# Retention and a low-rank mixer: the first two batches by pairs of heads, loads on two queues

## The chip, the cores and the metric

The kernel runs on one core of a Trainium2 chip. The time is the device time of one execution in microseconds. The core has a matrix engine (PE, whose weight loads are shown as PEld), a vector engine (DVE), a scalar engine (ACT), a general engine (POOL) and a sync engine (SP). Each takes its own instructions in program order, and they wait for one another by semaphores. DMAs are issued by SP, ACT or POOL and share 16 DMA engines.

## The reference

```python
B, H, S, D = 8, 8, 576, 64            # batch, heads, tokens, head width
scores = (1 / sqrt(D)) * q @ k^T
gamma  = 1 - 2 ** (-5 - h)            # one decay per head
ret    = scores * where(i >= j, gamma ** (i - j), 0)
x      = (ret @ v), heads side by side   # [B, S, 512]
h      = x^T @ U @ V                  # U [576, 32], V [32, 576]: mixes tokens
u      = x + h^T
out    = u + relu(u @ w_ch1) @ w_ch2  # w_ch1 [512, 2048], w_ch2 [2048, 512]
```

All inputs and the output are float32; the kernel computes its products in bf16.

## The kernel before

Retention runs by chunks of 128 tokens. Within a chunk k and q are transposed, scores are multiplied and masked (`ret`), and `ret @ v` goes to `po`; from chunk to chunk a state (sum of k^T v) is carried, which q is multiplied with. The decay is put into factors: v is scaled by gamma^-t (`vscale`) and the result by gamma^t (`qscale`) as x is written. 576 tokens are four and a half chunks, so two batches share nine chunks; the middle one, J, holds the last 64 tokens of the even batch and the first 64 of the odd one.

Then, for a batch: `a` = U^T x (MA), u^T (for batch 0 built as x^T plus V^T a; for the others as a transpose of u), u = x + h (MH), y1 = relu(u w_ch1) kept transposed, 16 blocks of four or five chunks (`Y1`, L477), and y2 = y1 w_ch2 plus u (`Y2`, L511), stored from POOL's queue.

Batches 2 to 7 are woven into the y1 and y2 of the batch before them by a fixed merge, and load, cast and transpose by DMA ahead of their use. The first two batches have a hand-written order instead, and only this order is touched:

- `startup` (L779) does batch 0 up to its u^T. The unit is 256 tokens with all eight heads; each tensor of a unit is two loads of 256 KB (four heads each), all from SP. A token pair lies side by side in a partition, so that k and q are transposed with even and odd tokens apart. POOL casts k and q to bf16 (L592) and scales v (L596). `T_u` transposes on PE, DVE or ACT copies; `SC_u` makes scores of four heads, `mask_u` masks them on DVE (L643); `ST_u` sums states, which ACT copies to `sblk` as block-diagonal pairs (L697); `RV_u` and `QS_u` add into `po`; `XS_u` writes x. `T_J`, `SC_J` and so on do the half chunk. At the end stand 16 x^T matmuls (L859), MA of all four 128-column blocks, four matmuls V^T a (L874) and the four copies to u^T (L882).
- `warm(n)` puts n matmuls on the identity, 512 columns wide, into the order; 21 in all.
- `early_consts` is called ahead of everything: identity, masks, decay factors; ACT computes three exponentials there.
- `first_stretch` (L886) then runs the 16 y1 items of batch 0 (`y(n)` gives n of them) with batch 1's two units between them, `MA1`, MH and the transposes `MT1`, and begins y1 of batch 1.

Buffers: stage (float32 loads) 15; in PSUM one buffer each for `psc`, `po` and `pss` (states, MA), and three for `big` (transposes, x^T, y1, y2). DMAs from SP and ACT use eight completion semaphores in turn, and an issue waits until the DMA eight before it in program order has landed.

Of the kernel before, what the change touches and what calls it, by code (L numbers as in the profile page):

```python
# [35 lines left out]
def kernel(  # L36
# [23 lines left out]
    J = 4  # L60
# [35 lines left out]
    vscaleU = consts.tile([P, 4, 2, H], FP32, name="vscaleU")  # L96
# [17 lines left out]
    def early_consts():  # L114
# [21 lines left out]
        nc.scalar.activation(out=vscaleU, in_=posU, func=AF.Exp, bias=lnb, scale=-1.0)  # L136
# [21 lines left out]
    def load_u_rows():  # L158
        nc.sync.dma_start(
            out=U_f[:, 0:4, :], in_=moe_U[0:4 * P, :].rearrange("(c p) r -> p c r", p=P))  # L160
        nc.sync.dma_start(out=U_f[0:HALF, J, :], in_=moe_U[4 * P:S, :])

    def load_v_rows():
        nc.sync.dma_start(out=V_f, in_=moe_V)

    def make_u():
        nc.scalar.activation(out=U_E[:, 0:J, :], in_=U_f[:, 0:J, :], func=AF.Copy)
        nc.scalar.activation(out=U_E[0:HALF, J, :], in_=U_f[0:HALF, J, :], func=AF.Copy)

        ps = ps_s.tile([P, 5, R], FP32, tag="pss", name="pu_o")  # L170
        nc.tensor.matmul(ps, swap, U_E, start=True, stop=True)
        nc.scalar.activation(out=U_O[0:HALF, 1:5, :], in_=ps[0:HALF, 0:4, :], func=AF.Copy)
        nc.scalar.activation(out=U_O[HALF:P, :, :], in_=ps[HALF:P, :, :], func=AF.Copy)
# [59 lines left out]
    def cast_qk(pr, i, rows=slice(0, P), eng=None):  # L233
# [4 lines left out]
        if eng is not None:  # L238
            for j in (1, 0):
                eng.tensor_copy(  # L240
                    out=t[rows, j, :], in_=c["f", j][rows].rearrange("p h d -> p (h d)"))
            return
# [222 lines left out]
    def y1_items(par, by_seg=False):  # L465
        nch = 4 + par
        segs = [(0, 4)] if par == 0 else [(0, 3), (3, 2)]
        items = []

        def Y1(f, seg):  # L470
            if f == 0 and seg == 0:
# [88 lines left out]
    un = [dict() for _ in range(4)]  # L560
    st["x", 0] = x_pool.tile([P, NI, dm], BF16, tag="x", name="xt")

    def unit_i0(u):
        return 2 * u + (1 if u >= 2 else 0)

    def load_u(u, which):
        b = u // 2
        t0 = 2 * P * (u % 2) + HALF * b
        for j in which:
            dram = (q, k, v)[j]  # L570
            for hh in range(2):
                t = stage.tile([P, H, D], FP32, tag="stage", name="stage_t")
                un[u]["f", j, hh] = t
                nc.sync.dma_start(  # L574
                    out=t.rearrange("p (h j) d -> p h (j d)", j=2),
                    in_=dram[b, 4 * hh:4 * hh + 4, t0:t0 + 2 * P, :].rearrange(
                        "h (p j) d -> p h (j d)", j=2),
                )

    def unit_views(u, j, hh):  # L580
        if j not in un[u]:
            un[u][j] = qk_pool.tile([P, 2, dm], BF16, tag="qk", name="qk")
        w = slice(hh * 4 * D, (hh + 1) * 4 * D)
        return (un[u][j][:, :, w].rearrange("p j (h d) -> p h j d", d=D),
                un[u]["f", j, hh].rearrange("p (h j) d -> p h j d", j=2))

    def cast_u(u, j, hh, eng):
        o, f = unit_views(u, j, hh)
        if eng is nc.scalar:
            nc.scalar.activation(out=o, in_=f, func=AF.Copy)  # L590
        else:
            eng.tensor_copy(out=o, in_=f)  # L592

    def scale_u(u, hh, eng):
        o, f = unit_views(u, 2, hh)
        eng.tensor_tensor(  # L596
            out=o, in0=f,
            in1=vscaleU[:, u, :, 4 * hh:4 * hh + 4].rearrange("p j h -> p h j")[
                :, :, :, None].to_broadcast([P, 4, 2, D]),
# [3 lines left out]
    def T_u(u, j, eng):  # L603
        pst = ps_big.tile([P, 2 * NHP, P], BF16, tag="big", name="pst")
        for jj in range(2):
            for hp in range(NHP):
                nc.tensor.transpose(
                    pst[:, jj * NHP + hp, :], un[u][j][:, jj, hp * P:(hp + 1) * P], ident)
        t = qkT_pool.tile([P, 2 * NHP, P], BF16, tag="qkT", name="qkT")
        un[u]["T", j] = t  # L610
        o, i_ = t, pst
        if j == 0:

            o = t.rearrange("p a b -> p (a b)").rearrange(
                "p (hp t j) -> p j hp t", hp=NHP, j=2)
            i_ = pst.rearrange("p (j hp) t -> p j hp t", j=2)
        if eng is nc.scalar:
            nc.scalar.activation(out=o, in_=i_, func=AF.Copy)
        else:
            eng.tensor_copy(out=o, in_=i_)  # L620

    def qT(u):
        return un[u]["T", 0].rearrange("p a b -> p (a b)").rearrange(
            "p (hp t) -> p hp t", hp=NHP)

    def SC_u(u, hh, pool_, tag):
        psc = pool_.tile([P, 2, NHP, P], FP32, tag=tag, name="psc")
        kT, qt = un[u]["T", 1], qT(u)
        for hp in range(2):
            for jj in range(2):  # L630
                for s in range(2):
                    for hl in range(2):
                        r = slice(hl * HALF, (hl + 1) * HALF)
                        m = slice(s * HALF, (s + 1) * HALF)
                        nc.tensor.matmul(  # L635
                            psc[m, hl, hp * 2 + jj, :], kT[r, jj * NHP + 2 * hh + hp, m],
                            qt[r, 2 * hh + hp, s * P:(s + 1) * P], start=True, stop=True,
                        )
        un[u]["psc", hh] = psc

    def mask_u(u, hh):
        ret = ret_pool.tile([P, H, P], BF16, tag="ret", name="ret")
        nc.vector.tensor_tensor(  # L643
            out=ret.rearrange("p (a j) i -> p a (j i)", j=2),
            in0=un[u]["psc", hh].rearrange("p a b i -> p (a b i)").rearrange(
                "p (a ji) -> p a ji", a=4),
# [3 lines left out]
        un[u]["ret", hh] = ret  # L650

    def RV_u(u, hh):
        if "po" not in un[u]:
            un[u]["po"] = ps_o.tile([P, 2, dm], FP32, tag="po", name="po")
        for hp in range(2):
            for hl in range(2):
                h = 4 * hh + 2 * hp + hl
                for jj in range(2):
                    for s in range(2):
                        r = slice(s * HALF, (s + 1) * HALF)  # L660
                        nc.tensor.matmul(  # L661
                            un[u]["po"][:, s, h * D:(h + 1) * D],
                            un[u]["ret", hh][r, hl * 4 + hp * 2 + jj, :],
                            un[u][2][r, jj, h * D:(h + 1) * D],
                            start=(h == 0 and jj == 0), stop=True, skip_group_check=True,
                        )

    def QS_u(u, s, slot):
        for hp in range(NHP):
            nc.tensor.matmul(  # L670
                un[u]["po"][:, s, hp * P:(hp + 1) * P],
                qT(u)[:, hp, s * P:(s + 1) * P], sblk[:, slot, hp, :],
                start=False, stop=True, skip_group_check=True,
            )

    def XS_u(u, c0=0, c1=2):
        i0, n = unit_i0(u) + c0, c1 - c0
        nc.vector.tensor_tensor(  # L678
            out=st["x", 0][:, i0:i0 + n, :].rearrange("p s (h d) -> p s h d", d=D),
            in0=un[u]["po"][:, c0:c1, :].rearrange("p s (h d) -> p s h d", d=D),  # L680
            in1=qscale[:, i0:i0 + n, :, None].to_broadcast([P, n, H, D]), op=ALU.mult,
        )

    def ST_u(u, rows, acc, start):
        for hp in range(NHP):
            for jj in range(2):
                nc.tensor.matmul(  # L687
                    acc[:, hp, :], un[u][1][rows, jj, hp * P:(hp + 1) * P],
                    un[u][2][rows, jj, hp * P:(hp + 1) * P],
                    start=(start and hp == 0 and jj == 0), stop=True,  # L690
                    skip_group_check=True,
                )

    def Sblk(acc, slot):
        for hl in range(2):
            r = slice(hl * HALF, (hl + 1) * HALF)
            nc.scalar.activation(  # L697
                out=sblk[r, slot, :, hl * D:(hl + 1) * D],
                in_=acc[r, :, hl * D:(hl + 1) * D], func=AF.Copy)

    LO, HI, ALL = slice(0, HALF), slice(HALF, P), slice(0, P)

    def T_J(r):
        c = ch[0, J]
        pst = ps_big.tile([P, 2 * NHP, P], BF16, tag="big", name="pst")
        for j in range(2):
            for hp in range(NHP):
                nc.tensor.transpose(
                    pst[:, j * NHP + hp, r], c["qk"][r, j, hp * P:(hp + 1) * P],
                    ident[r, r])  # L710
        if "qkT" not in c:
            c["qkT"] = qkT_pool.tile([P, 2 * NHP, P], BF16, tag="qkT", name="qkT")
        nc.scalar.activation(out=c["qkT"][:, :, r], in_=pst[:, :, r], func=AF.Copy)

    def SC_J(r):
        c = ch[0, J]
        c["psc"] = ps_sc.tile([P, 2, NHP, P], FP32, tag="psc", name="psc")
        for hp in range(NHP):
            for hl in range(2):
                d = slice(hl * HALF, (hl + 1) * HALF)  # L720
                nc.tensor.matmul(
                    c["psc"][r, hl, hp, r], c["qkT"][d, NHP + hp, r], c["qkT"][d, hp, r],
# [3 lines left out]
    def mask_J(r):  # L726
        c = ch[0, J]
        if "ret" not in c:
            c["ret"] = ret_pool.tile([P, H, P], BF16, tag="ret", name="ret")
        nc.vector.tensor_tensor(  # L730
            out=c["ret"].rearrange("p (hp hl) i -> p hl hp i", hl=2)[r, :, :, r],
            in0=c["psc"][r, :, :, r],
            in1=tri[r, None, None, r].to_broadcast([HALF, 2, NHP, HALF]), op=ALU.mult,
        )

    def RV_J(r):
# [277 lines left out]
```

## Time and profile before

| | |
|---|---|
| median of 3 runs | 335.97 us (334.06 to 337.58) |
| span of the profiled execution | 335.6 us, clock 0.974 on average |
| first y1 matmul of batch 0 starts | 32.1 us |
| first y1 matmul of batch 1 starts | 61.2 us |
| first y2 matmul | 82.1 us |
| idle of PE between 50 and 60, 60 and 70 us | 1.0, 1.2 us |
| PE busy from 100 us to the end | 231.1 of 235.6 us |

The span goes from the first to the last instruction of one profiled execution. A line of a timeline or chain gives start and length in us, engine, program line, operation, and output <- input; `x20` says that 20 instructions were merged, and the brackets at the end give idle time before it and what ended that. A line of windows gives a stretch, its length, busy time and instructions of PE, PEld, DVE, ACT and POOL, the granted PE clock (1.00 is full), the DMA engines' busy share and GB/s. `SPq` is SP's issuing of DMAs.

### The profile page before, as it was taken

The page shows a single profiled execution, that of the slowest core. Times are in us where ns is not written, and L with a number is a line of the kernel's source. Part 1 is how long each engine was busy: PE and PEld are TensorE (multiplying, and loading weights), DVE is VectorE, ACT ScalarE, POOL GpSimd, SP SyncE. Part 2 cuts the span into 40 slices and gives each one's busy share as a digit, 9 for nine tenths or more (in the row PEclk, how much of TensorE's full clock was granted, in tenths as well). Part 3 has the DMA queues.
Part 4 walks back from the last instruction along what each step waited for, and adds up shares of the span by engine and source line. Part 5 has one row for each costly group of instructions (what it writes and reads, how often), then busy time and mean ns, then how long its engine had stood idle before and what let it go on. Part 6 is the DMA issues. An engine that isn't in the chain of part 4 may idle for free.

```text
span 335.6 us, 6997 instructions
## 1 busy us (share of the span) xinstructions
PE 320.9 (96%) x2926; PEld 179.9 (54%) x2948; DVE 138.0 (41%) x190; ACT 139.2 (41%) x290; POOL 78.2 (23%) x112
## 2 busy tenths in 40 slices
PE   6688999899999999999999999999999999999996
PEld 3375554576544445446764455457754455457644
DVE  5453346433564234534356244524365144510022
ACT  2543665776210077107850176017740264037400
POOL 5686741211231140114102220222111100110000
PEclk9955999999999999999999999999999999999999
DMA  7999999999999929994998959995933400340012
GB/s 212 239 228 266 237 217 182 187 179 223 213 249 234 234 73 192 207 198 105 198 177 190 213 123 168 195 241 71 200 76 99 142 2 1 79 126 2 0 64 94
DMA packets 151311, 53.17 MB, mean 158 GB/s; under 512 B 131984, under 2 KB 148752, under 8 KB 151280
## 3 DMA queue, kind: packets, MB, share of 16 engines
q1 hardware_dynamic: 144512, 40.40, 64.7%
q0 software_dynamic: 6768, 12.32, 14.6%
q8 instruction: 23, 0.38, 0.5%
q14 instruction: 8, 0.07, 0.1%
HBM read 36.85 MB, written 9.44 MB: 138 GB/s over the span
## 4 chain that ended last, share of the span: by engine, by line
PE 91%; SPq 2%; issue 2%; DVE 2%; DMA 1%; ACT 1%; POOL 0%
PE ps_y L477 38%; PE ps_y L511 36%; PE psc L275 3%; PE po L314 2%; PE pss L687 2%; PE pss L340 2%; DMA stage_t<-in_q_dram 1%; SPq L574 1%; PE ph L421 1%; PE ps_y L522 1%; PE pa L394 1%; PE po L300 1%; PE po L661 1%; PE xT L859 1%; DVE xt L678 1%
## 5 line engine op out<-in xcount | busy, mean ns | idle before, releaser
L477 PE MATMUL ps_y<-uT,w_sb 128*128 128x256 bf16 (+2 forms) x768 | 137.0, 328 | 1.5 <-ACT uT L452 1.4
L482 ACT ACTIVATE y<-ps_y 128x384 bf16<-128x384 f32 (+2 forms) x192 | 90.0, 489 | 114.9 <-PE ps_y L477 114.2
L511 PE MATMUL ps_y<-w_sb,y 128*128 128x512 bf16 x538 | 124.3, 379 | 1.6 <-issue 0.8
L477 PEld LDWEIGHTS <-w_sb 128*128 128x128 bf16 x768 | 71.6, 98 | 46.7 <-issue 3.1
L511 PEld LDWEIGHTS <-y 128*128 128x128 bf16 x560 | 52.4, 98 | 60.3
L500 DVE TENSOR_TENSOR o_sb<-ps_y,u 128x512 f32<-128x512 f32 (+2 forms) x38 | 25.2, 663 | 76.6 <-PE ps_y L511 74.4
L503 POOL DMA_DIRECT2D out_dram<-o_sb x31 | 17.3, 558 | 158.6 <-DVE o_sb L500 152.8
L285 DVE TENSOR_TENSOR ret<-psc,tri 128x1024 bf16<-128x1024 f32 x24 | 29.4, 1225 | 47.3 <-PE psc L275 47.3
L254 POOL TENSOR_TENSOR vt<-stage_t,vscale 128x512 bf16<-128x512 f32 (+1 forms) x29 | 30.0, 1047 | 50.6 <-DMA stage_t<-in_v_dram 50.1
L325 DVE TENSOR_TENSOR xt<-po,qscale 128x512 bf16<-128x512 f32 x27 | 18.6, 691 | 25.9 <-PE po L314 25.9
L427 DVE TENSOR_TENSOR u<-ph,xt 128x768 bf16<-128x768 f32 (+2 forms) x24 | 21.8, 951 | 13.5 <-PE ph L421 13.5
L348 ACT ACTIVATE s_sb<-pss 128x512 bf16<-128x512 f32 x24 | 14.3, 597 | 8.3 <-PE pss L340 7.3
L245 ACT ACTIVATE qk<-stage_t 128x512 bf16<-128x512 f32 x27 | 16.5, 622 | 2.1 <-DVE o_sb L500 2.1
L243 DVE CAST qk<-stage_t 128x512 bf16<-128x512 f32 x27 | 16.3, 604 | 0.0
L400 ACT ACTIVATE a_sb<-pa 128x128 bf16<-128x128 f32 x8 | 2.2, 276 | 33.0 <-PE pa L394 33.0
L643 DVE TENSOR_TENSOR ret<-psc,triU 128x1024 bf16<-128x1024 f32 x8 | 9.7, 1222 | 11.3 <-PE psc L635 11.3
L314 PEld LDWEIGHTS <-ret 128*128 128x128 bf16 x216 | 10.0, 98 | 4.2
L592 POOL CAST qk<-stage_t 128x512 bf16<-128x512 f32 x16 | 9.6, 611 | 7.0 <-DMA stage_t<-in_q_dram 5.3
L275 PEld LDWEIGHTS <-qkT 64*128 64x128 bf16 x216 | 6.1, 94 | 9.1 <-issue 8.7
L275 PE MATMUL psc<-qkT 64*128 64x128 bf16 x216 | 10.7, 219 | 0.0
L314 PE MATMUL po<-vt,ret 128*128 128x64 bf16 x216 | 10.7, 193 | 0.0
L340 PE MATMUL pss<-vt,qk 128*128 128x128 bf16 (+1 forms) x96 | 9.3, 219 | 0.0
(103 smaller groups left out, 165.5 us busy)
## 6 DMA issues: line engine op xcount, KB each, us to landing
stage_t<-in_k_dram SPq DMA_DIRECT2D x32, 256.0 KB, 4.1
stage_t<-in_q_dram SPq DMA_DIRECT2D x32, 256.0 KB, 4.9
stage_t<-in_v_dram SPq DMA_DIRECT2D x32, 256.0 KB, 5.5
out_dram<-o_sb POOLq DMA_DIRECT2D x31, 256.0 KB, 3.8
w_sb<-in_moe_w_ch_dram POOLq DMA_DIRECT2D x4, 512.0 KB, 8.4
w_sb<-in_moe_w_ch_dram POOLq DMA_DIRECT2D x8, 256.0 KB, 10.2
stage_t<-in_k_dram SPq DMA_DIRECT2D x8, 128.0 KB, 4.2
stage_t<-in_q_dram SPq DMA_DIRECT2D x8, 128.0 KB, 4.0
```

Of the source, the lines that this page charges most:

```text
L245: nc.scalar.activation(out=t[rows, 0, :], in_=c["f", 0][rows].rearrange("p h d -> p (h d)"), func=AF.Copy)
L254: (eng or nc.gpsimd).tensor_tensor(out=c["v"][rows], in0=c["f", 2][rows], in1=vscale[rows, i, :, None].to_broadcast([n, H, D]), op=ALU.mult,)
L275: nc.tensor.matmul(psc[:, hl, hp, :], qkT[r, NHP + hp, :], qkT[r, hp, :], start=True, stop=True,)
L285: nc.vector.tensor_tensor(out=ret.rearrange("p (hp hl) i -> p hl hp i", hl=2), in0=c["psc"], in1=m[:, None, None, :].to_broadcast([P, 2, N ...
L314: nc.tensor.matmul(c["po"][:, hl, hp * D:(hp + 1) * D], c["ret"][:, h, :], c["v"][:, h, :], start=(first and hp == 0), stop=True, skip_gro ...
L325: nc.vector.tensor_tensor(out=xt[:, i, :].rearrange("p (hp hl d) -> p hl hp d", hl=2, d=D), in0=c["po"][:, :, 0:NHP * D].rearrange("p hl ( ...
L427: nc.vector.tensor_tensor(out=st["u", par][:, i0 - base:i0 - base + n, w].rearrange("p s (c d) -> p c s d", c=2), in0=ph[k][:, :, 0:n, :], ...
L477: nc.tensor.matmul(ps[:, 0:n, :], w1_sb[:, cc, f * P:(f + 1) * P], st["uT", par][:, c0:c0 + n, cc, :], start=(cc == 0), stop=(cc == NCC - 1),)
L482: nc.scalar.activation(out=st["y1", par][:, f, c0 * P:(c0 + n) * P], in_=ps[:, 0:n, :].rearrange("p s t -> p (s t)"), func=AF.Relu)
L500: nc.vector.tensor_tensor(out=o_sb[:, 0:n], in0=ps[:, 0:n], in1=st["u", par][:, c, w], op=ALU.add)
L503: (nc.sync if last else nc.gpsimd).dma_start(out=out_flat[r0:r0 + P, w], in_=o_sb[:, 0:n])
L511: nc.tensor.matmul(ps, st["y1", par][:, f, c * P:(c + 1) * P], w2_sb[:, f, :], start=(f == 0), stop=(f == NF - 1),)
```

## The change

The first two batches go by pairs of heads (`hp`, 0 to 3) over all 512 tokens of a batch's whole chunks, instead of by 256 tokens over all heads. Each pair has its own loads, casts, transposes, scores, mask, state, `po`, x, x^T, MA block (32 rows of `a`) and u^T block. k, q and v of a pair are 256 KB each, loaded as two DMAs of 128 KB.

- In `startup`, q of batch 0, the first J tiles, V and U are issued from ACT, the others from SP. `early_consts` now stands behind the first six loads, and the exponential for v is four instructions.
- Of the 21 `warm` matmuls the first ten stay; 14 `dummy` matmuls of the same shape are put in front of scores (4, 2, 2, 2) and states (2, 2).
- `ST_h` makes all states of a pair as running sums: the rows of an earlier chunk are added into every later state at once (64, 192 columns wide). J's rows of batch 1 are added into all four.
- Batch 1's u^T is built like batch 0's, by x^T plus V^T a on PE, instead of by MH and transposes of u; its J chunk by `UT_J`. MH for both batches (u itself, needed by y2) comes later, between y1 items of batch 1.
- `make_u` is split: U's even form in `startup`, the odd form in `first_stretch`.
- The loads of chunks of batches 2 and 3, the w2 loads and batch 1's first y1 items stand in a new order.

```diff
 def load_u_rows():
-    nc.sync.dma_start(
+    nc.scalar.dma_start(
...
+def load_h(b, hp, j, eng):
+    t0 = HALF * b
+    t = stage.tile([P, H, D], FP32, tag="stage", name="stage_t")
+    for u in range(2):
+        eng.dma_start(out=t.rearrange("p (u h j) d -> p u h (j d)", u=2, h=2)[:, u],
...
+def T_h(b, hp, ek, eq, n=0):
+    pst = ps_big.tile([P, 2 * NHP, P], BF16, tag="big", name="pst")
...
+    copy(ek, c["kT"], pst[:, 0:4, :])
+    copy(eq, c["qT"].rearrange("p (u t j) -> p u j t", u=2, j=2), ...
+def SC_h(b, hp, n=0):
+    psc = ps_sc.tile([P, 2, 4, P], FP32, tag="psc", name="psc")
+    dummy(psc[:, 0], n)
...
+def ST_h(b, hp, engs, n=0):
+    acc_t = ps_s.tile([P, 4, P], FP32, tag="pss", name="acc")
+    dummy(acc_t, n)
...
+def MA_h(b, hp, eng):
+    g = slice(hp * R, (hp + 1) * R)
+    pa = ps_s.tile([P, P], FP32, tag="pss", name="pa")
+    for n in range(5):
+        nc.tensor.matmul(pa[g, :], (U_E if b == 0 else U_O)[:, n, :],
...
+def UT_h(b, hp, engs):
+    nc.tensor.matmul(t, st["a", b][g, :], V4[g, c0:c0 + 4 * P],
+        start=False, stop=True, skip_group_check=True)
...
 def startup():
+    load_h(0, 0, 1, nc.sync)
+    load_h(0, 0, 0, nc.scalar)
+    load_h(0, 0, 2, nc.sync)
+    load_h(0, 1, 1, nc.sync)
+    load_h(0, 1, 0, nc.scalar)
+    load_h(0, 1, 2, nc.sync)
+    early_consts()
+    load_J(0, nc.scalar)
+    load_v_rows()
+    load_u_rows()
...
+    load_h(0, 2, 0, nc.scalar)
...
+    load_h(0, 3, 0, nc.scalar)
...
+    warm(10)
+    pool_h(0)
+    T_h(0, 0, V, A)
+    SC_h(0, 0, 4)
+    mask_h(0, 0)
+    pool_h(1)
+    T_h(0, 1, V, A)
+    ST_h(0, 0, (A, A), 2)
+    SC_h(0, 1, 2)
+    RQ_h(0, 0)
+    XS_h(0, 0)
+    mask_h(0, 1)
...
+    T_h(0, 2, V, A)
+    J_h(0)
+    XT_h(0, 0)
+    MA_h(0, 0, A)
+    SC_h(0, 2, 2)
+    mask_h(0, 2)
+    pool_h(3, True)
+    load_w1(0)
+    J_h(1)
+    XT_h(0, 1)
+    MA_h(0, 1, A)
+    UT_h(0, 0, (A,))
+    ST_h(0, 2, (A, A))
...
+    SC_h(0, 3, 2)
+    mask_h(0, 3)
+    scale_h(0, 3, nc.gpsimd, slice(0, 1))
+    scale_h(0, 3, nc.vector, slice(1, 2))
...
+    RQ_h(0, 3)
+    XS_h(0, 3)
+    J_h(3)
+    XT_h(0, 3)
+    MA_h(0, 3, A)
+    UT_h(0, 3, (A, V))
...
 def first_stretch():
...
+    for hp in range(NHP):
+        cast_h(1, hp, 1, nc.gpsimd)
+        cast_h(1, hp, 0, nc.gpsimd)
+        scale_h(1, hp, nc.gpsimd)
+        T_h(1, hp, V, A)
+        if hp:
+            XT_h(1, hp - 1)
+            MA_h(1, hp - 1, V)
+        y(1)
+        SC_h(1, hp)
+        mask_h(1, hp)
+        ST_h(1, hp, (A, A))
+        y(1)
+        if hp:
+            UT_h(1, hp - 1, (V,))
+        y(1)
+        RQ_h(1, hp)
+        XS_h(1, hp)
     for f in range(0, NF, 2):
         load_w2(f)
+    XT_h(1, 3)
+    MA_h(1, 3, A)
+    UT_J(0, A)
     y(16)
+    UT_h(1, 3, (A, V))
+    UT_J(2, A)
```

`RQ_h` is `ret @ v` (16 matmuls of 64 columns) and q times state (three or four of 128) for one pair into one `po`; `XS_h` writes x in two instructions; `J_h` does the pair's part of J; `XT_h` is four x^T matmuls.

## The prediction

> **What bounds the kernel now.** I read the page's busy table first, then its slices for the granted clock, then the chain that ended last over the first 36 us, then each engine's timeline there, and last the built instruction order of the changed kernel, which lists the semaphores that each instruction waits for.
>
> ```profile
> PE 320.9 (96%) x2926; PEld 179.9 (54%) x2948; DVE 138.0 (41%) x190; ACT 139.2 (41%) x290; POOL 78.2 (23%) x112
> PEclk9955999999999999999999999999999999999999
> ```
>
> TensorE is the bound, and the only slow stretch is slices 3 and 4. From the first y1 matmul (32.1 us) on, matmuls follow one another nearly without gaps, so the change can win or lose in two places: the time to that matmul, and the first stretch behind it.
>
> ```profile
> 8.98 4.91 DMA stage_t<-in_q_dram
> 13.94 0.62 POOL qk L240
> ...
> 16.55 1.72 DVE qk L596
> 18.32 2.40 PE pss L687 x20
> 20.72 0.96 PE po L661 x30
> ...
> 27.75 1.39 PE xT L859 x12
> 29.14 0.65 PE pa L394 x17
> ...
> 30.92 0.59 ACT uT L882
> ...
> 32.14 1.82 PE ps_y L477 x4
> ```
>
> Columns are start, length, what. Loads end the waits up to 14 us; from 18.3 us on PE works almost without a pause. It works at half clock, as three half-microsecond windows show (the figure before the DMA share):
>
> ```profile
> 17.50:18.00 0.50, 0.00 (x0) 0.00 (x0) 0.50 (x1) 0.00 (x0) 0.43 (x2) 0.81 1.07 96
> 28.50:29.00 0.50, 0.50 (x7) 0.38 (x4) 0.00 (x0) 0.00 (x0) 0.00 (x0) 0.50 1.15 339
> 34.50:35.00 0.50, 0.50 (x3) 0.17 (x2) 0.50 (x1) 0.09 (x1) 0.50 (x1) 0.62 1.14 206
> ```
>
> The clock fell at 17.8 us after PE pauses of at most 1.8 us, stayed at 0.50 while PE was over 90% busy with small matmuls, and returned at 34.9 us, 2.8 us after 512-column matmuls began.
>
> **Loads on two queues.** The windows show a DMA share of 1.13 to 1.24 between 5 and 30 us: the engines are full, and a second queue brings bytes no faster. What it does add is work on ACT, which is in order:
>
> ```profile
> 0.74 0.99 SPq L574 DMA_DIRECT2D stage_t<-in_k_dram  x2
> 2.24 1.28 ACT L136 ACT_TABLE_LOAD   x1 [2.24 <-DVE posU L133]
> 8.39 1.31 ACT L618 ACTIVATE qkT<-pst 128x1024 bf16<-128x1024 bf16 x1 [4.12 <-PE pst L607]
> ```
>
> ACT was free for the first q^T copy at 8.4 us. In the new order 14 DMA issues stand ahead of that copy: four halves of q, three J tiles, V, two of U, four more halves of q. Issues cost 0.50 us on SP (0.65 for J tiles), and the program uses eight completion semaphores in turn, so an issue also waits until the one eight before it, on either queue, has landed. The fourth waits for the first half of q. The first 256 KB landed at 3.8 us before; two halves on two queues come to the same bytes, so it is issued at 3.9 to 4.4. Table load 1.28 and six exponentials of 0.25 (three took 3.53 to 4.28): 7.2. Ten issues, 3 x 0.65 + 7 x 0.5 = 5.5: 12.7. The last of them also waits for the second U piece, issued near 10 and landing some 2 us or more later. I take ACT free at 13.0; 11.2 with issues of 0.42 and no wait, 15 with the 0.84 to 0.93 that U's issues took on SP.
>
> Who waits: the first pair's scores need q^T. PE does the first transposes at about 6, four dummies until 7.3, and stands until 13.75 (ACT 13.0 plus 0.75, half of L618's 1.31 and its start). POOL is not held: its casts go on behind the loads (pairs 0, 1 and J by about 12.6, pair 3 by 18), and w1's first block is issued at about 18, landing 8.4 later by its median, well ahead of y1. That cover is good for 15 us.
>
> The Trainium skill (DMA: Bandwidth & Descriptors, "Issuing engines are not separate DMA queues") says that issuing from several engines saves only sequencer time, which speaks against this change. It puts no price on what ACT loses.
>
> **The chain by pairs.** From 13.75 on nearly all data is there, and PE's list sets the pace. At half clock, from rows of that stretch: a 128-column matmul 0.12 (L687: 2.40/20), a 64-column one 0.032 (L661: 0.96/30), a 512-column one 0.45 (L477: 1.82/4). Per pair: transposes 8 x 0.12 = 0.95; scores, 16 small, 0.5 (0.35 to 0.7; 0.35 at full clock); state, 12 of 64 and 4 of 192 columns, 0.95 (0.6 if its two column halves overlap, 1.1 if not); RQ 16 x 0.032 + 3 x 0.12 = 0.87; J part 0.2; XT 0.48; MA 5 x 0.12 = 0.6; UT 0.45. That is 5.0, times four, less the first transposes: 19.0. J's own transposes and scores and the V product add 1.1, ten remaining dummies 4.5. Sum 24.6, against 13.2 between 18.3 and 31.5 before: u^T no longer goes four at a time in different array rows (L874 took 0.54 for four), dummies are added, and each pair pays its own state and MA.
>
> Waits come on top, since scores, po and states have one buffer each. J's copy and V_b on ACT: 1.2. MA of pair 1 behind the 1.22 mask of pair 2 on DVE, because J's x follows that mask: 0.9. MA of pair 2 behind mask 3 and half of v's scale: 1.5. State 3 behind the a copy: 0.35. Last pair: XS before XT 0.65, a 0.35, last copy 0.5. Together 5.5. So y1 begins at 13.75 + 24.6 + 5.5 = 43.8. If the clock falls only at 17.8 as before, 2.0 less; I take the middle, 42.8, which is 10.7 later than 32.1.
>
> At full clock PE's list halves to 12.3, but other engines are then last: a pair passes kT 0.4, q^T 0.75, mask 1.22, two x writes 0.75, a 0.25, u^T 0.6, in order behind other pairs' work. Stepping through the order, scores start at 13.75, 16.6, 23.4 and 28.1, and y1 at 35.1.
>
> **Do the dummies keep the clock?** Before, 21 were spread and the clock fell anyway; now 10 open the kernel and 14 stand ahead of scores and states, with PE idle for 6.4 us after the first four. I take it as fallen by the restart. After it, two dummies (0.9) per 3 us with small matmuls resemble 18 to 31 us more than the y1 stretch that brought the clock back. The Trainium skill (TensorE: Matmul & The Clock Gate, "The HAM clock gate") says that some 3.4 us of sustained activity restores full rate. By that rule the clock would return near 17 and y1 would start near 37, a total of about 343. The rows differ: 13 us at over 90% busy did not restore it, so my sum goes by the rows.
>
> **The first stretch.** Full-clock prices: 0.056 per 128 columns, 0.24 per 512. Added: XT 16 x 0.056 = 0.9, UT 4 x 0.24 = 1.0, UT_J 12 x 0.056 = 0.7, MA in one column strip 1.1 against 0.65, U_O 0.1. Removed: 20 transposes, 1.1. States about equal. Net +2.0. New waits: XT behind XS (0.8 on DVE against 0.43 of transposes) 3 x 0.37, then 0.8 and 0.3 after the last pair, 0.4 at the first q^T, 0.3 before Y1 of batch 1: 2.9. Those before, 55 to 62 us, come to 2.2 and go. Sum +2.7, from 0 (waits covered) to +5. The w2 loads and later q, k, v loads move behind batch 1's casts, to about 45; y2 needs w2 near 95. MH only moves. After this the program is the same.
>
> **Sum.** 335.6 + 10.7 + 2.7 = 349.0 as a span; the median of the runs before is 0.4 above the span, within their spread (334.06 to 337.58).
>
> **Rivals.** (1) Full clock, ACT still held: 335.6 + 3.0 + 2.7 = 341. For it: before, the clock survived to 17.8 on sparse work. Against: the idle 6.4 us. (2) A return midway, since work is piled up when ACT is free: half of the difference, 345. (3) Not slower: ACT's issues go through without waits and early enough that pair 0 runs at 7.5 us at full clock, as the change means it. Loads then gate (pair 2's at about 15), y1 starts at 29.7, total 335.6 - 2.4 + 2.7 = 336. It decides if ACT is free before about 9 us; against it stand fourteen issues of 0.5. Only with a first stretch at no cost as well is it faster, 332. (4) Nothing is gained by two queues and nothing lost: covered by (3) at 336.
>
> **Chances.** Half clock 0.5, midway 0.2, full clock with ACT held 0.18, rival 3 0.12, of which 0.05 faster. Measurements of this kernel tell about 1%, 3.4 us, from no change: faster 0.05, within 0.09 (rest of rival 3, the low end of rival 1), slower 0.86. Range: low end 338, rival 1 with ACT free at 11.2 (1.8 less) and a first stretch of about +1.2; high end 355, the forecast with ACT at 15 (+2.0), the first stretch at +5 (+2.3), states unoverlapped (4 x 0.15) and the clock down from the restart (+1.0).
>
> **What would show it.** ACT: DMA issues until about 13 us, first q^T copy behind them. PE: no matmul from 7 to 13. Clock at 0.5 from before 18 until after y1's start near 43. First stretch 2 to 3 us longer. I am wrong if the first score matmul runs by 9 us, or the clock stays at 1.0 through the pairs, or y1 begins before 33.

## The result and the profile after

| | before | after |
|---|---|---|
| median of 4 runs, side by side (us) | 336.77 (334.06 to 339.05) | 354.87 (354.3 to 357.68) |
| span of the profiled execution | 335.6 | 353.6 |
| first y1 matmul of batch 0 | 32.07 | 43.76 |
| first y1 matmul of batch 1 | 61.18 | 78.44 |
| first y2 matmul | 82.09 | 99.49 |
| first y1 matmul of batch 2 | 116.59 | 134.55 |

The changed kernel is slower: ratio 1.055, 95% interval 1.047 to 1.063. Of the 18.0 us between the two spans, 11.7 are there when the first y1 matmul starts; 6.3 more come between that matmul and y1 of batch 2; behind it the kernels run alike (219.0 us each to the end). These figures compare one profiled execution of each kernel, and the one of the kernel before was slow at its start: its mean clock is 0.974, where 55 other executions of that kernel, run beside the experiments, have 0.978 to 1.00.

The page of the changed kernel, its busy row of engines and its row of granted clocks:

```profile
PE 333.2 (94%) x2992; PEld 182.9 (52%) x3015; DVE 141.3 (40%) x217; ACT 139.5 (39%) x300; POOL 78.3 (22%) x113
PEclk9685579999999999999999999999999999999999
```

TensorE (PE; likewise VectorE is DVE, ScalarE ACT, SyncE SP) is busy 12 us longer on 66 more matmuls. Before, the third and fourth slices were at half clock; now the second (0.6) is slow as well, the third (0.8) much less so, and the fourth to sixth are at 0.5 to 0.7: the clock fell, came back and fell again (the trace puts the falls at 11.41 and 25.06, the returns at 18.24 and 48.96 us).

ScalarE's timeline of the changed kernel, start, length, instruction; ACTq is its issuing of DMAs:

```profile
0.74 3.36 ACTq L578 DMA_DIRECT2D stage_t<-in_q_dram  x4
4.20 1.28 ACT L138 ACT_TABLE_LOAD   x1 [4.20 <-DVE triJ L152]
5.49 0.90 ACT L138 ACTIVATE vscaleU<-posU,lnb 128x16 f32<-128x16 f32 x4
...
6.44 0.75 ACTq L733 DMA_DIRECT2D stage_t<-in_k_dram  x1
...
9.75 0.53 ACTq L166 DMA_DIRECT2D U_f<-in_moe_U_dram  x1
10.81 3.45 ACTq L578 DMA_DIRECT2D stage_t<-in_q_dram  x4
14.30 0.74 ACT L587 ACTIVATE qkT<-pst 128x512 bf16<-128x512 bf16 x1 [7.51 <-DMA stage_t<-in_v_dram]
```

Fourteen issues stand ahead of the first q^T copy, as the prediction stepped through them; it starts at 14.30 instead of 8.4 in the kernel before. The chain of waits up to the first y1 shows who paid (start, length, what):

```profile
7.91 4.91 DMA stage_t<-in_v_dram
...
12.84 0.37 ACTq L578
...
13.78 0.48 ACTq L578
...
14.30 0.75 ACT qkT L587
15.09 0.64 PE psc L643 x16
...
36.49 0.68 DVE vt L604
37.17 0.21 DVE xt L795
37.42 0.70 PE pa L817 x5
...
42.22 0.66 PE pa L817 x5
42.90 0.28 ACT a_sb L587
...
43.22 0.60 PE xT L838
```

The chain starts with J's v load. ScalarE's twelfth issue could not go until that load had landed at 12.8, and the first scores could not go until ScalarE was through. Three windows of one microsecond (busy times of PE, PEld, DVE, ACT and POOL, then clock, DMA share, GB/s) show TensorE's state:

```profile
12.00:13.00 1.00, 0.00 (x0) 0.00 (x0) 0.00 (x0) 0.00 (x0) 0.31 (x2) 0.50 0.65 172
19.00:20.00 1.00, 1.00 (x37) 0.72 (x36) 0.00 (x0) 0.25 (x1) 0.98 (x3) 1.00 0.72 162
31.00:32.00 1.00, 1.00 (x16) 0.91 (x10) 0.00 (x0) 0.66 (x2) 0.00 (x0) 0.50 1.20 216
```

At 12 us it has nothing to do; at 19 us it works off what has piled up, at full clock; at 31 us it is as busy with fewer than half the matmuls, at half clock.

### The profile page after: what moved, and what is told of

The parts are those of the page before. It is cut to its first block, busy times and chain, and to the rows that moved or that the text cites. A ratio compares the mean times of both kernels' runs of the same rounds, so it can differ in the third digit from the quotient of the medians.

```text
span 353.6 us, 7221 instructions
## 1 busy us (share of the span) xinstructions
PE 333.2 (94%) x2992; PEld 182.9 (52%) x3015; DVE 141.3 (40%) x217; ACT 139.5 (39%) x300; POOL 78.3 (22%) x113
## 4 chain that ended last, share of the span: by engine, by line
PE 90%; DMA 2%; ACT 2%; DVE 2%; issue 1%; ACTq 1%; DVEq 0%
PE ps_y L483 36%; PE ps_y L517 34%; PE psc L280 3%; PE po L319 2%; PE pss L345 2%; PE acc L668 1%; DMA stage_t<-in_v_dram 1%; PE pa L817 1%; PE ph L426 1%; PE psc L643 1%; PE ps_y L528 1%; PE xT L838 1%; PE po L305 1%; PE po L701 1%; DMA stage_t<-in_q_dram 1%
## 5 line engine op out<-in xcount | busy, mean ns | idle before, releaser
L259 POOL TENSOR_TENSOR vt<-stage_t,vscale 128x512 bf16<-128x512 f32 x27 | 28.2, 1053 | 56.3 <-DMA stage_t<-in_v_dram 51.1
L432 DVE TENSOR_TENSOR u<-ph,xt 128x1024 bf16<-128x1024 f32 (+2 forms) x24 | 21.8, 951 | 13.6 <-PE ph L426 13.6
L353 ACT ACTIVATE s_sb<-pss 128x512 bf16<-128x512 f32 x24 | 14.3, 596 | 10.1 <-PE pss L345 9.0
L248 DVE CAST qk<-stage_t 128x512 bf16<-128x512 f32 x27 | 15.5, 576 | 0.0
L589 POOL CAST qk<-stage_t 128x512 bf16<-128x512 f32 (+1 forms) x20 | 12.0, 614 | 12.4 <-DMA stage_t<-in_q_dram 7.9
L643 PE MATMUL psc<-qkT 64*64 64x128 bf16 x128 | 4.0, 255 | 8.9 <-ACT qkT L587 8.9
L587 ACT ACTIVATE qkT<-pst 128x512 bf16<-128x512 bf16 x8 | 5.9, 741 | 15.8 <-DVE qkT L589 8.3
```

Of the source, the lines that this page charges most:

```text
L259: (eng or nc.gpsimd).tensor_tensor(out=c["v"][rows], in0=c["f", 2][rows], in1=vscale[rows, i, :, None].to_broadcast([n, H, D]), op=ALU.mult,)
L432: nc.vector.tensor_tensor(out=st["u", par][:, i0 - base:i0 - base + n, w].rearrange("p s (c d) -> p c s d", c=2), in0=ph[k][:, :, 0:n, :], ...
```

## The experiments

All times are medians, with the kernel before run on the same chip; milestones are from each run's profile. The theory under test is the prediction's: ScalarE's issues and the half clock set the start, added TensorE work lengthens the first stretch.

**All loads on one queue.** The changed kernel with the loads that ScalarE issued moved to SyncE, in their place in the order.

```diff
-        load_h(0, 0, 0, nc.scalar)
+        load_h(0, 0, 0, nc.sync)
...
-        load_J(0, nc.scalar)
+        load_J(0, nc.sync)
```

> The changed kernel with every load issued from SP, in the same program order; ACT issues no DMA. If ACT's fourteen issues hold the chain, the first q^T copy comes at about 7 us instead of 14.3, the first scores at about 7.5 instead of 15.1, and y1 starts 5 to 8 us earlier than 43.8, more if the clock then never falls: 345 to 350 us. If instead the order of the pairs on DVE and PE sets the end, or the data, y1 moves by under 2 us: 353 to 355.

347.95 us against 337.45, ratio 1.030 (1.022 to 1.038). The first q^T copy starts at 6.95, first scores at 7.74, first y1 at 36.77: 7.0 us earlier than in the changed kernel, and the span is 7.8 shorter. Nothing but the issuing engine is changed, so this much is ScalarE's issuing. The clock still falls (16.3) and returns only at 40.2, behind the start of y1.

**TensorE kept busy while ScalarE issues.** 34 dummies instead of 4 ahead of the first scores.

```diff
-        SC_h(0, 0, 4)
+        SC_h(0, 0, 34)
```

> The changed kernel with 34 instead of 4 dummies ahead of the first scores, so that PE is busy from 6 to about 13 us, while ACT is held as before. If the fallen clock is the larger part, it now stays at 1.0 through the first pairs, and y1 starts near 36.4 (the 35.1 worked out at full clock, plus 1.3 as ACT was free at 14.3 and not 13.0): about 347 us. If the hold on ACT alone matters, the time stays at 354 to 355; if the clock falls again once the first scores run, 350 to 354.

353.14 us, ratio 1.050 (1.040 to 1.059). The clock holds to 22.6 instead of 11.41, falls for 3.4 us, and falls again from 36.3 to 43.1. First y1 comes at 40.01, 3.75 us earlier. This profile is the fastest of its four executions; over the four the mean clock is 0.962 to 0.985, against 0.947 to 0.961 in the changed kernel. So the clock answers to how TensorE is fed, and it has a price; but a start that was waited for until 15 us isn't bought back with it here.

**No dummies.** All 14 taken out of the changed kernel.

> The changed kernel without its 14 dummies ahead of scores and states; nothing of the result is left out. If they only add to PE's list (0.45 each at half clock, ten of them on the chain, partly beside waits), y1 starts 2 to 4 us earlier: 351 to 353 us. If they are what brought the clock back from 18.2 to 25.1 us, the clock stays at 0.5 from 11 us to after y1's start, and y1 starts 1 to 3 us later: 356 to 358.

354.22 us, ratio 1.050 (1.043 to 1.056), and the clock stays at 0.50 from 10.6 to 48.1. Still first y1 is 2.0 us earlier (41.78). So in the profile of the changed kernel the dummies brought the clock back for 6.8 us (18.24 to 25.06), and took more from the chain than that gave. Over four executions each the mean clock is 0.946 to 0.952 without them and 0.947 to 0.961 with them. At the end of the first stretch 1.4 us of it are left. In the medians (354.22 against 354.87) no difference is shown.

**The first stretch alone.** The kernel before with its own start and the changed kernel's `first_stretch` behind it.

> The startup of before, with batch 1 in the changed form behind it: loads, casts, transposes, states, x^T, MA and u^T by pairs, later MH; U's odd form stays in startup. If the changed first stretch has a cost of its own (5.7 us between first y1 and first y2, of which about 1.2 come from the clock returning later), this is 4 to 5 us slower than before: about 341. If the cost came only from the late and slow startup, it is within 1 us of before.

339.55 us, ratio 1.007 (1.003 to 1.010). First y1 at 31.53 and y1 of batch 2 at 120.00 are 88.47 us apart, against 84.52 before: 3.95 more, and in this run the clock was back before y1 began, which before it was not until 2.8 us later. The stretch's loss is there without the new start, but the profile overstates it: it is the slowest of ten executions, and by the medians the loss is 2.1 us (339.55 against 337.45), less than the 4 to 5 that were expected.

Adding up TensorE's groups between the two marks, start to start and less the waits, gives (us, this run against before): transposes of x 2.18 and u^T 1.26, both new; J's u^T 1.50, new; the mixer's first product 1.54 against 0.65; transposes of q and k 2.51 against 1.79; states 2.30 against 1.69; the transposes of u that go, 0 against 1.38; `ret @ v`, scores and MH 3.86 against 4.37. That is 5.3 us more, the waits come to 1.34 against 2.34, and the y1 matmuls take 0.8 less, since none of them runs at half clock. But merged lines hide short waits. A pair's part reads so in the changed kernel's timeline, with the weight loads (PEld) and VectorE's writes of x:

```profile
61.79 0.76 DVE L717 TENSOR_TENSOR xt<-po,qscale 128x256 bf16<-128x256 f32 x2 [0.95 <-PE po L709]
62.27 0.11 PEld L828 LDWEIGHTS <-xt 128*128 128x128 bf16 x2 [0.24 <-DVE xt L717]
62.27 0.62 PE L828 MATMUL xT<-ident,xt 128*128 128x128 bf16 x4
62.60 0.11 PEld L828 LDWEIGHTS <-xt 128*128 128x128 bf16 x2 [0.22 <-DVE xt L717]
62.82 0.45 PE L817 MATMUL pa<-xt,U_O 128*32 128x128 bf16 x5
```

Four 128-column matmuls take 0.55 us from their start to the next group's, 0.14 each, at full clock. They are not one row: the first two wait 0.24 us for VectorE's first write of x, which lengthens the group of q and k transposes ahead of them, and the other two wait 0.22 us for the second write. In the run of the stretch alone the weight loads' waits for x are, in us, times and longest:

```profile
PEld L1047 <- DVE xt L936: 2.3, 8, 0.7
```

The longest, 0.7, is the last pair's, which the 1.34 hold already. So some 1.6 of the 5.3 us are waits for x: the added work is some 3.7, and the waits are some 2.9 against 2.34.

**The stretch with x used later.** In the run before, the transposes of x and the mixer's first product go behind the y matmuls that followed them.

```diff
             T_h(1, hp, V, A)
+            y(1)
             if hp:
                 XT_h(1, hp - 1)
                 MA_h(1, hp - 1, V)
-            y(1)
```

> The kernel before's start with the changed kernel's first stretch (the run of the stretch alone), and in its loop over pairs the transposes of x and the mixer's first product moved behind the y matmuls that followed them, so that the writes of x have 1.8 us more before TensorE asks for them. Theory (the stretch's added 5 us are TensorE's work: transposes of x 2.2, u^T 1.3, J's u^T 1.5, the mixer's first product 0.9, states 0.6, against 1.4 and some others that go): no change from the stretch alone, first y1 to y1 of the second batch 88 to 89 us, time 338.5 to 340.5. Rival (waits for the writes of x and of the masks): three iterations lose 0.4 to 0.5 us each, 87 us between the same two marks and 337.5 to 338.5.

339.43 us, ratio 1.009 (1.006 to 1.012): no change from the stretch alone. From first y1 to first y2 it takes 52.35 us against 53.41, and a pair's part now reads:

```profile
44.73 0.43 PEld L1047 LDWEIGHTS <-xt 128*128 128x128 bf16 x4
44.94 0.39 PE L1047 MATMUL xT<-ident,xt 128*128 128x128 bf16 x4
45.26 0.45 PE L1036 MATMUL pa<-xt,U_O 128*32 128x128 bf16 x5
```

The same four matmuls take 0.32 to the next group's start. Over the four pairs the transposes of x take 1.49 us instead of 2.18 and those of q and k 1.80 instead of 2.51; the first product takes 0.3 more. So the waits for x are real, and the move is worth 1.1. It is not seen in the time. In this execution the clock came back at 21.1, first y1 began 3.05 us earlier (28.48), and with that and the 1.1 TensorE reached y1 of batch 2 early, only to wait 2.6 us for a DMA, the transpose of u. The expected 88 to 89 or 87 between the marks can't be read any more (90.1 with that wait). That wait is new, and the next run meets it again.

**The kernel before with TensorE kept busy.** More warm-up matmuls where the kernel before pauses ahead of 18 us.

```diff
-        warm(3)
+        warm(5)
...
-        warm(2)
+        warm(6)
...
-        warm(2)
+        warm(9)
         T_J(LO)
...
+        warm(4)
...
         ST_u(0, LO, accA, True)
```

> The kernel before with more warm-up matmuls where TensorE pauses ahead of 18 us: 5 instead of 3 and 6 instead of 2 around the first transposes, 9 instead of 2 ahead of J's transposes, 4 new ones ahead of the first states. Theory (the clock is a price that any order of this start pays, and the fall at 17.8 us comes from TensorE's pauses): the clock stays at full speed from 18 us on, the 13 us of half-speed work halve where no wait stands in, first y1 starts at 26 to 29 us instead of 32.1, and the time is 330 to 333, faster than the kernel before by 1 to 2%. Rival (the work ahead of first y1 is bound by VectorE, ScalarE and GpSimd, or the clock falls all the same): first y1 at 31 to 33 and 335 to 339, no change.

In its profile the clock stays at full speed from the first to the last slice and first y1 starts at 27.89, 4.2 us earlier than in the profile of the kernel before; the time is the same: 335.99 against 335.94, ratio 1.000 (0.996 to 1.003). Neither outcome had been foreseen. TensorE's waits between 50 and 125 us in this run (who waited for whom, us in total, times, longest):

```profile
PE psc L275 <- DMA qkT<-qk: 3.2, 1, 3.2
PE ps_y L477 <- ACT uT L452: 1.9, 2, 1.4
PE ps_y L477 <- DMA uT<-u: 0.8, 1, 0.8
PE ph L421 <- DVE u L427: 0.6, 1, 0.6
PE ps_y L477 <- ACT y L482: 0.6, 1, 0.6
```

In this execution the gain is handed back in waits, the largest for a transpose by DMA of a next batch's q and k, and y1 of batch 2 begins at 116.51, where it began before (116.59). That an earlier start is of no use at all isn't shown. The kernel before loses less to the clock than its profile says: the median of the mean clocks of the 23 executions beside this run is 0.99, of these twelve 0.995. The difference is 3.4 us of half clock, an estimated 1.7 us of start, where the interval of the ratio is 1.3 us wide to either side. And among the 55 other executions of the kernel before, the 25 with a mean clock of 0.994 or more have a median of 335.6 us, the eight with 0.98 or less 337.3. The runs show only that the 1 to 2% expected are not to be had.

**More bytes.** The kernel before with two of the eight w2 loads issued twice.

```diff
         for f in range(0, NF, 2):
             load_w2(f)
+        for f in (0, 2):
+            load_w2(f)
```

> The kernel before with two of its eight w2 loads issued a second time behind the eighth (512 KB each, same bytes to the same place): 1.05 MB more for the DMA engines at about 46 to 60 us. Theory (until batch 2's y1 at 116.6 us the DMA engines are as full as TensorE, so that a start that is earlier, as in the run of the kernel before with TensorE fed, is taken back by waits for loads): 1.05 MB at 224 GB/s are 4.7 us; batch 2's y1 at 119 to 122, time 338 to 341. Rival (the loads have slack, and what took back the earlier start is something else): batch 2's y1 at 116.5 to 117, time 335 to 337.

339.6 us against 336.35, ratio 1.009 (1.005 to 1.014): slower as the theory said, but not by its mechanism. In the profile y1 of batch 2 starts at 117.09, 0.5 later than before and not 2.4 to 5.4:

```profile
117.09 2.90 PE L477 MATMUL ps_y<-uT,w_sb 128*128 128x512 bf16 x8 [1.96 <-DMA uT<-u]
```

TensorE came early here as well (first y1 at 30.39) and waited 1.96 us for u^T; the first eight matmuls then took 2.90 us where they take 1.89 in the kernel before, since the clock fell right behind the wait (0.50 from 118 to 121). In three runs y1 of batch 2 waits for this transpose of u: to 116.51 with TensorE fed, to 117.09 here, to 118.62 with x used later. That it is the bytes, at 224 GB/s, is not shown: 4.7 us of them moved the mark by 0.6 (from 116.51). What makes this run slower stays open.

**q of two pairs on ScalarE.** The changed kernel with its first four ScalarE issues kept and the other ten moved to SyncE.

```diff
-        load_J(0, nc.scalar)
+        load_J(0, nc.sync)
...
-        load_h(0, 2, 0, nc.scalar)
+        load_h(0, 2, 0, nc.sync)
```

> The changed kernel with only the four q loads of the first two pairs left on ScalarE; J's, the mixer's U and V and q of pairs 2 and 3 go from SyncE in the same order. Theory (what costs is that issues behind the fourth stand on ScalarE until a semaphore of an earlier load is free, ahead of its first copy): ScalarE is done with issues at 4 us, its first copy starts at 7 to 8 us, first scores at 8 to 9, first y1 at 36 to 38 us, time 347 to 350, like the run with all loads on SyncE. Rival (a second queue by itself slows the first loads or their landings): first copy still after 10 us, first y1 at 39 to 42, 350 to 353.

347.59 us against 335.94, ratio 1.032 (1.028 to 1.037); first y1 at 35.93. ScalarE's timeline of this run:

```profile
0.74 3.40 ACTq L578 DMA_DIRECT2D stage_t<-in_q_dram  x4
...
7.17 0.74 ACT L587 ACTIVATE qkT<-pst 128x512 bf16<-128x512 bf16 x1 [0.34 <-DVE qkT L589]
```

The four early issues put off ScalarE's exponentials, from 2.2 to 4.2 us, and its first copy by 0.2 (6.95 with all loads on SyncE), and SyncE is four issues shorter. So a second queue is harmless by itself (ratio 1.032, against 1.030 with all loads on SyncE); the ten issues that stand between ScalarE and its first copy cost 7.8 us at first y1 (43.76 less 35.93).

**One queue, TensorE kept busy.** All loads on SyncE, and 4, 6, 4 and 4 dummies ahead of the first states, J's scores and the scores of pairs 2 and 3.

> The changed kernel with the loads that ScalarE issued on SyncE's queue, in the same order, and more dummies where TensorE paused: 4 instead of 2 ahead of the first pair's states, 6 ahead of J's scores, 4 instead of 2 ahead of the scores of pairs 2 and 3. It asks what the order by pairs costs once ScalarE is free and the clock is held. Theory (the start's loss is ScalarE's issues, 7.0 us, and a clock at half speed for 24 us): if the added work holds the clock past 24 us, first y1 starts at 31 to 34 us and the time is 341 to 345, slower than the kernel before by the first stretch's work alone (about 4 to 5 us). Rival (the clock falls for another reason than TensorE's pauses): it falls at 16 to 17 us as in the run with the loads moved, first y1 at 36.8 or, with the added matmuls at half speed, 38, and 348 to 350.

346.32 us, ratio 1.028 (1.023 to 1.032). Between the two theories: the clock holds to 24.3, then is lost from 24.3 to 27.7 and from 31.1 to 41.4. First y1 at 36.09, 0.7 earlier than without the dummies, and the span is no shorter (346.0 against 345.8): what they bought they mostly cost.

**The same from two pairs' q, first try.** The run with q of two pairs on ScalarE, the dummies of the last run without pair 3's, and 1, 4, 4 and 1 more ahead of the mixer's first products, where TensorE waits for x.

```diff
-        pa = ps_s.tile([P, P], FP32, tag="pss", name="pa")
+        pa_t = ps_s.tile([P, 4, P], FP32, tag="pss", name="pa")
+        dummy(pa_t, n)
+        pa = pa_t[:, 0, :]
```

> The run with q of two pairs on ScalarE and the other loads on SyncE, with more dummies: 4 instead of 2 ahead of the first pair's states, 6 ahead of J's scores, 4 instead of 2 ahead of pair 2's scores, and 1, 4, 4 and 1 ahead of the mixer's first products of the four pairs, where TensorE waited for x (0.24, 0.96 and 1.30 us in the run with dummies before). It asks what is left of the start's loss when neither issues nor the clock hold it. Theory (the clock falls for TensorE's pauses; fed, it stays): clock at full speed to 30 us at least, first y1 at 32 to 33.5, time 342 to 345: the order by pairs then starts y1 as late as the kernel before, and 5 us of first stretch are left. Rival (the chain of pairs, not the clock, sets first y1): clock held and y1 still at 35 to 36, time 345.5 to 347.5, as without the added dummies.

347.17 us, ratio 1.028 (1.025 to 1.032); the clock holds to 34.4, yet first y1 starts at 35.05. By its numbers that is the rival. TensorE's timeline shows why the run doesn't prove it:

```profile
20.63 0.40 PE L831 MATMUL xT<-ident,xt 128*128 128x128 bf16 x4
22.00 1.02 PE L614 MATMUL pa<-ident 128*128 128x512 bf16 x4 [0.97 <-DVE xt L796]
```

The four dummies stand behind the wait instead of in it. Their buffer, the only one of its kind, was still being read for J's part of x, so they added 1.0 us to the chain here and again at pair 2.

**The same with the dummies ahead of the transposes of x.** 1, 4 and 5 for pairs 0 to 2 go into the buffer of the transposes, 2 instead of 4 ahead of pair 2's scores.

```diff
     t = ps_big.tile([P, dm], FP32, tag="big", name="xT")
+    dummy(t, n)
```

> The run before (q of two pairs on ScalarE, TensorE fed) with its dummies ahead of the mixer's first products moved ahead of the transposes of x, 1, 4 and 5 for pairs 0 to 2, and 2 instead of 4 ahead of pair 2's scores. In the run before the 1 + 4 + 4 + 1 stood behind the wait for x, since they needed the same buffer, and so lengthened the chain by some 2.8 us; the 2 extra ahead of the scores by 0.5. It asks once more what sets first y1 at full clock. Theory (the clock, once dummies fill pauses and add nothing): clock held to 30 us, first y1 at 31.5 to 33, time 342 to 344. Rival (the chain of scores, masks and x itself, whatever the dummies): clock held and first y1 at 34 to 35.5, time 345 to 347. If the clock falls before 27 us, it tells nothing.

342.9 us (341.6 to 343.46) against 335.51, ratio 1.023 (1.018 to 1.027). The clock row of its page, and the same place in its timeline:

```profile
PEclk9999999999999999999999999999999999999999
```

```profile
19.42 1.04 PE L614 MATMUL xT<-ident 128*128 128x512 bf16 x4
20.29 0.39 PE L830 MATMUL xT<-ident,xt 128*128 128x128 bf16 x4
20.78 0.44 PE L818 MATMUL pa<-xt,U_E 128*32 128x128 bf16 x5
```

No wait is left between the three groups, and first y1 starts at 31.47, at the low end of what the theory gave: 4.5 us earlier than with the same loads and half clock (35.93), and earlier than in the kernel before. The profiled execution is the fastest of its four (341.6) and the only one with a mean clock of 1.00; the others have 0.99 to 0.995, so that in them the clock fell for 3.4 to 6.8 us, and take up to 1.9 us more. With the same loads and fewer dummies all four had 0.960 to 0.965, and the median was 347.59.

## What the prediction had right, and which steps failed

It forecast 349.0 us, slower with 0.86; 354.87 is at the upper edge of its range (355). Direction and mechanism were right: ScalarE's issues hold the start, half clock lengthens it, and the first stretch grows. Of the 18.0 us between the spans 13.4 were forecast. Of the 4.6 that are missing, 1.0 lie ahead of y1 and 3.6 in the first stretch, whose sum is the term that failed: +2.7 was forecast and +6.3 measured. The step that the clock stays at half speed from the restart to y1 failed too, without much effect on the number. Its steps:

**Loads on two queues: right, 1.3 us short.** The mechanism is shown by two runs: the same loads issued elsewhere give back 7.0 us, and the ten late issues account for it. ScalarE was free at 14.3, taken at 13.0 within 11.2 to 15. The walk through the eight semaphores let the last issue wait for the second U piece, at a cost of 0.3 us; the waits were on J's k, which held the eleventh issue to 10.81, and on J's v, which landed at 12.8 and held the twelfth. SyncE stood too: its timeline has no issue between 8.22 and 11.62, and the DMA share was 0.65 at 12 us, where the prediction took it as full. The Trainium skill (DMA: Bandwidth & Descriptors, "Issuing engines are not separate DMA queues") says that issuing from several engines saves only sequencer time. The run with four issues agrees that little is saved that y1 would see (35.93 against 36.77). What the change paid is another matter: 7.8 us at first y1, because an engine that works in order had work of its own behind the issues.

**The chain by pairs: right in sum, partly by luck.** y1 was put at 42.8 (43.8 if the clock fell at the restart) and came at 43.76. The clock did not fall once and stay: it returned 3.1 us after TensorE's restart, for 6.8 us, and fell again. The prediction had that as a rival, worth 345 in all, and as the skill's rule (TensorE: Matmul & The Clock Gate, "The HAM clock gate"), which lets about 3.4 us of sustained activity restore the full rate. This return agrees with the rule. What followed doesn't: from 31.89 to 35.30 TensorE was busy without a pause, as it was from 21.23 to 24.64 in the kernel before, and both times the clock stayed at 0.50. Nor does the rule's other half, a fall after an idle window of some 3.4 us: in the kernel before the clock fell after pauses of 1.8 us at most, and with 17 more wide matmuls it didn't fall in the profile. "I take it as fallen by the restart" came true (11.41), but half clock from there to y1 failed as a step, while the sum held because the half clock was still there in 18.7 of the 25.5 us between 18.24 and 43.76, because ScalarE came 1.3 later, and because the prices were low: in the run without dummies, at half clock throughout, it is 27.3 us from the first scores to y1 (14.49 to 41.78), where the forecast's terms without the dummies give 25.6. That these errors cancel is luck.

**Do the dummies keep the clock: not these, but others do.** Fourteen in the changed places bought 6.8 us of full clock and in the profiles cost 2.0 us of start. Placed where TensorE paused anyway they held it throughout in one execution of four and nearly so in the others, and then were worth 4.5 us in the profiles and 4.7 in the medians (347.59 and 342.9).

**The first stretch: mis-sized, and the largest error.** +2.7 was forecast with 0 to +5 as its bounds; +6.3 came. The term that failed is its work of +2.0, which is some 3.7 in the run of the stretch alone, and the groups take the same times in the changed kernel. J's u^T took 1.50 instead of 0.7, u^T 1.26 instead of 1.0, the transposes of x some 1.3 without their waits instead of 0.9, the first product 0.9 more instead of 0.45, and "states about equal" hid 0.6; the scores, which took less, and the transposes of u give 0.8 back. The new waits were sized right: 2.9 forecast, some 2.9 measured, against 2.2 and 2.34 that go; a good half of them stand in merged lines. Another 1.2 or so lies in the clock, which returned 5.2 us after y1's start instead of 2.8, and which the forecast of this stretch left out. J's transposes and U's odd form, which now stand behind y1's start, are most of the rest. By the medians of its two runs the stretch costs less behind the old start, 2.1 us and 3.5 (339.43 against 335.94); why less is not shown.

**Rivals.** "Not slower", which needed ScalarE free before 9 us, was the right condition with the wrong price: with ScalarE's first copy at 7 us, y1 came at 36 and not at 29.7, since half clock was left out of it, and the whole at 1.03. With both, ScalarE free and full clock, y1 came at 31.5. Full clock with ScalarE held was not tried through to y1; with 34 dummies the clock still fell at 22.6.

By the spans of one profiled execution each, the 18.0 us come apart as 7.8 for late issues on ScalarE, 4.5 for the clock, less 0.6 for the order itself against a start before that also ran half clocked, and 6.3 in the first stretch. The 0.6 is less than profiles of one and the same start differ by (3 us, below). By the medians the first two are 7.3 (354.87 to 347.59) and 4.7, which leaves 6 to 7 for order and stretch. Against a start before at full clock (27.89) the order by pairs is 3.6 us later.

## What to carry to other kernels

Before a load is moved to another engine's queue, list what that engine does next and which loads its issues wait for: here four issues ahead of its first work cost nothing, and ten more, which waited for loads, cost 7 to 8 us. A filler matmul helped only where its buffer was free before the wait that it was to fill; read in the timeline on which side of the wait it went. In a merged line, ask the weight loads what they waited for before calling the time work. And before a start is made faster, look for the next mark that something else sets, and at the clocks of more executions than the profiled one: here a start 4 us earlier in its profile did not move the median, and one 11.7 us later cost all of it.

## What was not expected of the hardware

The granted clock changed on a grid: all distances between changes in the kernels before and after are multiples of 3.41 us (17.06 is five) within 0.03: 17.06, 6.83, 6.82 and 23.90, and the two falls of the changed kernel are four such steps apart. Where in the grid an execution starts differs: the same start was half clocked for 13.6 us in one run of the changed stretch and for 3.4 in the other, and first y1 moved from 31.53 to 28.48. A single profile of this kernel's start is therefore uncertain by 3 us, without any edit, and differences of 2 us and less between first y1 of two runs above show nothing by themselves.
